# GeGLU feed-forward on one core: the first token block's transposes move from TensorE to the DMA queues

## The chip, the cores and the metric

The kernel runs on one core of a Trainium2 chip. The metric is device time in microseconds (us) for one execution; a time is the median of several runs. The core has a matrix engine (TensorE, PE in the profile, with its weight loads shown as PEld), a vector engine (VectorE, DVE), a scalar engine (ScalarE, ACT), a general one (GpSimd, POOL), and a synchronising engine (SyncE, SP) that here does nothing but issue DMA transfers. ScalarE issues DMA transfers as well, on a queue of its own.

## The reference

```python
B, S, D, F = 1, 2048, 1024, 3584          # all bfloat16
def reference(x, w_gate, w_up, w_down):
    return (gelu(x @ w_gate) * (x @ w_up)) @ w_down    # gelu: tanh approximation
```

x is 2048 tokens by 1024; w_gate and w_up are 1024 by 3584; w_down is 3584 by 1024.

## The kernel before

**Tiling.** The tokens are worked on in two halves of 1024 (`h`), each of two blocks of 512 tokens (`tb`). For the first two matrix products TensorE needs x transposed: `xT[tb]` holds, for each of the eight blocks of 128 input columns (`kd`, `KD` = 8), 128 partitions by 512 tokens. The 3584 hidden columns are taken as 28 blocks of 128, in 14 pairs; a chunk of weights has 512 of them, for w_gate (`j` = 0) and w_up (`j` = 1). The gated result goes to `hT`, which the down product reads.

**Most of the work is Winograd's form of a 2 by 2 block product**: seven products m1 to m7 instead of eight. Its sums of weights (`s1` to `s4`, made by `s_sum`, mostly on GpSimd) and of inputs (`t1` to `t4`, made by `t_sum`, mostly on VectorE) are kept in a 4-byte format. `quads` does this for the gate and up products (matmuls on line 418) and `down_group` for the down product (line 698).

**The very first pair is done the plain way**, because the sums are not there yet: `first_pair_units` runs 32 matmuls for the first token block and 32 for the second (`part`, which calls `mm_gu`, line 267), eight blocks `kd` times two matrices times two units `u`. Their weights are the first 256 columns (`FA`) of the first chunk. Then `quads` follows with pair 1, in the order in which it is written.

**How the first data come in.** `load_x0` (line 166) brings the first token block in rows: column quarters 0 and 1 of four (`XQ` = 256 columns), as three transfers. `transpose_x0` (line 311) turns these into `xT[0]` blocks 0 to 3 with 16 transposes of 128 by 128 on TensorE against an identity matrix, into PSUM banks, and VectorE (line 319) and ScalarE (line 321) copy them out. Blocks 4 to 7 of `xT[0]`, and all of `xT[1]`, come by transposing DMA transfers (`load_xT`, line 171). `load_w` (line 160) loads weights on SyncE's or ScalarE's queue.

**What sets the order.** The helpers `sp`, `act`, `dve`, `pool` and `pe` tie each engine's instructions to the order in which the program writes them, so each queue can be read off the text. Transfers signal on a small set of completion counters that are used in turn; a transfer whose counter is still in use by an earlier one waits for that one to land. Ahead of all real work TensorE runs `NWARM` matmuls of constants (`warm`, line 202), 128 by 512 each, to no purpose but to be busy.

The order of the first transfers is, on SyncE: half of x quarter 0, w_gate blocks 0 and 1, w_up blocks 0 and 1, w_up blocks 2 to 4, then transposing transfers of block 4, block 5 and blocks 6 and 7 of the first token block, then three of the second token block, then the rest of the first weight chunk and the second chunk. On ScalarE: the other half of x quarter 0, x quarter 1, w_gate blocks 2 to 4, and then w_gate and w_up blocks 5 to 7, which are tied behind the first transposing transfer; behind them the load of the table for gelu (line 225).

In `first_pair_units` the plain matmuls are interleaved with the transposes: eight transposes, half a warm-up, the gate matmuls of blocks 0 and 1 (four), eight transposes, the up matmuls of blocks 0 and 1 (four), and then blocks 2 to 7 in order.

Of the kernel before, what the change touches and what calls it, by code (L numbers as in the profile page):

```python
# [7 lines left out]

ACT = mybir.ActivationFunctionType
ALU = mybir.AluOpType  # L10
BF16 = mybir.dt.bfloat16
F32 = mybir.dt.float32
F32R = mybir.dt.float32r
SCHED_DEP = mybir.DependencyInfo(
    mybir.DependencyClass.NoSync, mybir.DependencyReason.SCHED_ONLY
)
# [18 lines left out]
def kernel(  # L35
# [8 lines left out]
    nc = tc.nc  # L44
    P = 128
    x2 = x.flatten_outer_dims()
    out2 = out.flatten_outer_dims()
    S, D = x2.shape
    F = w_gate.shape[1]
    KD = D // P  # L50
    KH = KD // 2
    KF = F // P
    TB = 512
# [3 lines left out]
    FG = 512  # L57
# [1 line left out]
    DN = 512  # L59
    NDN = D // DN  # L60
    TSB = TB // P
    XQ = 256
    NXQ = D // XQ
    KPQ = XQ // P
    NWARM = 7
    NPAIR = KF // 2
    PPG = FPG // 2
    WDT = 2
# [8 lines left out]
    wuv = w_up.rearrange("(ko ki) f -> ki ko f", ki=P)  # L77
    wdv = w_down.rearrange("(ko ki) d -> ki ko d", ki=P)

    const_pool = ctx.enter_context(tc.tile_pool(name="const", bufs=1))  # L80
    xT_pool = ctx.enter_context(tc.tile_pool(name="xT", bufs=1))
    shared_pool = ctx.enter_context(tc.tile_pool(name="shared", bufs=1))
    hT_pool = ctx.enter_context(tc.tile_pool(name="hT", bufs=1))
# [15 lines left out]
    CH = KD * FG  # L99
    w_mem = shared_pool.tile([P, 4 * CH + (NS - 4) * DN], BF16, name="w_mem")  # L100
# [5 lines left out]
    banks = [psum.tile([P, TB], F32, name=f"bank{i}") for i in range(8)]  # L106
    PB, VB, QB, RB = (0, 1), (2, 3), (4, 5), (6, 7)
    last_on = {}

    def on(engine, inst):  # L110

        if engine in last_on:
            tc.add_manual_dep(
                inst.ins, last_on[engine].ins.name, SCHED_DEP, reason="engine order"
            )
        last_on[engine] = inst
        return inst

    def sp(inst):
        return on("sp", inst)  # L120

    def act(inst):
        return on("act", inst)

    def dve(inst):
        return on("dve", inst)
# [12 lines left out]
    def pe(inst):  # L139
        return on("pe", inst)  # L140


    xs0 = w_mem[:, 4 * CH : 4 * CH + TSB * D].rearrange("p (a b) -> p a b", b=D)
    chunks = {}

    def new_chunk(key):
        c0 = 2 * CH * (key[1] % 2)
        chunks[key] = tuple(
            w_mem[:, c0 + j * CH : c0 + (j + 1) * CH].rearrange(
                "p (a b) -> p a b", b=FG  # L150
            )
            for j in range(2)
        )

    def load_w(key, j, k0, k1, queue=sp, f0=0, f1=FG):

        c0 = key[1] * FG
        eng = nc.scalar if queue is act else nc.sync
        src = (wgv, wuv)[j][:, k0:k1, c0 + f0 : c0 + f1]
        queue(eng.dma_start(out=chunks[key][j][:, k0:k1, f0:f1], in_=src))  # L160

    def load_x0(q, queue, ts0=0, ts1=TSB):
        eng = nc.scalar if queue is act else nc.sync
        cols = slice(q * XQ, (q + 1) * XQ)
        src = x2[ts0 * P : ts1 * P, cols].rearrange("(ts p) d -> p ts d", p=P)
        queue(eng.dma_start(out=xs0[:, ts0:ts1, cols], in_=src))

    def load_xT(xT, h, tb, k0, k1):
        t0 = h * SH + tb * TB
        sp(  # L170
            nc.sync.dma_start_transpose(
                out=xT[tb][:, k0:k1, :],
                in_=xv[t0 : t0 + TB, k0:k1, :],
            )
        )
# [4 lines left out]
    xT = [None] * NTB  # L180
# [3 lines left out]

    FA = 2 * P
    first = (0, 0)
    load_x0(0, sp, 0, 2)
    load_x0(0, act, 2, TSB)
    load_w(first, 0, 0, 2, sp, 0, FA)
    load_x0(1, act)  # L190
    load_w(first, 1, 0, 2, sp, 0, FA)
    load_w(first, 0, 2, 5, act, 0, FA)
    load_w(first, 1, 2, 5, sp, 0, FA)
    ident = const_pool.tile([P, P], BF16, name="ident")
    make_identity(nc, ident[:])

    warm_l = nc.const_aps.tensor(1.0, [P, P], BF16)
    warm_r = nc.const_aps.tensor(1.0, [P, TB], BF16)
# [1 line left out]
    def warm(bank, n=TB):  # L200
        pe(
            nc.tensor.matmul(  # L202
                banks[bank][:, 0:n],
                lhsT=warm_l,
                rhs=warm_r[:, 0:n],
                start=True,
                stop=True,
            )
        )

    for i in range(NWARM):
        warm(i)

    load_xT(xT, 0, 0, KH, KH + 1)
    behind_transpose = last_on["sp"]
    load_xT(xT, 0, 0, KH + 1, KH + 2)
    for j in range(2):
        load_w(first, j, 5, KD, act, 0, FA)
        tc.add_manual_dep(
            last_on["act"].ins,  # L220
            behind_transpose.ins.name,
            SCHED_DEP,
            reason="engine order",
        )
    act(nc.scalar.preload_act_table(ACT.Gelu_apprx_tanh))
    load_xT(xT, 0, 0, KH + 2, KD)
    for k0, k1 in ((0, 2), (2, KH), (KH, KD)):
        load_xT(xT, 0, 1, k0, k1)
    for j in range(2):
        load_w(first, j, 0, KD, sp, FA, FG)  # L230
    new_chunk((0, 1))
    for j in range(2):
        load_w((0, 1), j, 0, KD)


    tsum = {}
# [4 lines left out]
    def t_sum(name, c0=0, c1=KH, on_pool=False):  # L241
        def b(j, l):
            return xT[l][:, j * KH + c0 : j * KH + c1, :]

        t0 = ("t1", "t2", "t3", "b22", "t4").index(name) * KH * TB
        t = t_mem[:, t0 : t0 + KH * TB].rearrange("p (a b) -> p a b", b=TB)
        tsum[name] = t
        t = t[:, c0:c1, :]
        if name == "b22":
            for c in range(c1 - c0):  # L250
                act(nc.scalar.copy(out=t[:, c, :], in_=b(1, 1)[:, c, :]))
            return
        in0, in1 = {
            "t1": lambda: (b(0, 1), b(0, 0)),
            "t2": lambda: (b(1, 1), tsum["t1"].bitcast(F32)[:, c0:c1, :]),
            "t3": lambda: (b(1, 1), b(0, 1)),
            "t4": lambda: (b(1, 0), tsum["t2"].bitcast(F32)[:, c0:c1, :]),
        }[name]()
        if on_pool:
            pool(nc.gpsimd.tensor_tensor(out=t, in0=in0, in1=in1, op=ALU.subtract))  # L260
            return
        dve(nc.vector.tensor_tensor(out=t, in0=in0, in1=in1, op=ALU.subtract))


    def mm_gu(ps, w_sb, fi, tb, kd):
        pe(
            nc.tensor.matmul(  # L267
                ps[:],
                lhsT=w_sb[:, kd, fi * P : (fi + 1) * P],
                rhs=xT[tb][:, kd, :],  # L270
                start=(kd == 0),
                stop=(kd == KD - 1),
            )
        )
# [24 lines left out]
    def unit_out(hT, bset, fi, tb):  # L299
        mult(hT, gelu(banks[bset[0]]), banks[bset[1]], fi, tb)  # L300

    def transpose_x0(q):

        parts = [(2 * q, 0, 4), (2 * q + 1, 0, 4)]
        if q == 0:
            parts = [(0, 0, 2), (0, 2, 4), (1, 0, 4)]
        for n, (kd, ts0, ts1) in enumerate(parts):
            tp = banks[(PB + QB)[(2 * q + n) % 4]][:].bitcast(BF16)
            for ts in range(ts0, ts1):
                pe(  # L310
                    nc.tensor.transpose(  # L311
                        tp[:, ts * P : (ts + 1) * P],
                        xs0[:, ts, kd * P : (kd + 1) * P],
                        ident[:],
                    )
                )
            cols = slice(ts0 * P, ts1 * P)
            if q == 0 or n == 0:
                dve(nc.vector.tensor_copy(out=xT[0][:, kd, cols], in_=tp[:, cols]))
            else:  # L320
                act(nc.scalar.copy(out=xT[0][:, kd, cols], in_=tp[:, cols]))

    def part(held, tb, k0, k1, us=(0, 1), js=(0, 1)):
        for kd in range(k0, k1):
            for j in js:
                for u in us:
                    mm_gu(banks[held[u][j]], chunks[first][j], u, tb, kd)

    def first_pair_units(hT):

        held = (VB, RB)
        transpose_x0(0)
        warm(RB[1], TB // 2)
        part(held, 0, 0, KPQ, js=(0,))
        transpose_x0(1)
        part(held, 0, 0, KPQ, js=(1,))
        part(held, 0, KPQ, KD)
        t_sum("t1", 0, KH // 2)
        t_sum("t1", KH // 2, KH)
        for u in range(2):  # L340
            unit_out(hT, held[u], u, 0)
        held = (QB, PB)
        part(held, 1, 0, KH)
        t_sum("t2")
        t_sum("b22")
        t_sum("t3", 0, KH // 2)
        part(held, 1, KH, KD, (0,))
        unit_out(hT, held[0], 0, 1)
        t_sum("t3", KH // 2, KH)
        part(held, 1, KH, KD, (1,))  # L350
        unit_out(hT, held[1], 1, 1)
        for j in range(2):
            s_sum(0, 1, j, "s3", True, False)
        for name in ("s1", "s2", "s4"):
            for j in range(2):
                s_sum(0, 1, j, name)
# [711 lines left out]
```

## Time and profile before

| | |
|---|---|
| median of three runs | 539.03 us (538.97 to 539.69) |
| span of the profiled execution | 537.4 us |
| what lies around the span, if that execution took the median | 1.6 us |
| TensorE busy | 533.6 us, 99% |
| VectorE, ScalarE, GpSimd busy | 367.6, 263.5, 252.2 us |
| first warm-up matmul starts | 0.77 us |
| first plain matmul (line 267) starts | 4.93 us |
| first Winograd matmul (line 418) starts | 19.66 us |

A line of the chain has a start and a length in us, the engine, the tile and the line of the kernel, and how many instructions were merged. A line of the timeline has start, length, engine, line, operation, what is written and read, shapes and count; in brackets stands the idle time ahead and what ended it. A source line of a transfer has the duration of issuing it (smallest, median, largest, in ns) and when it was issued; "to landing" is from the start of the issue to the last completion. A line of a queue has packets, MB and busy share; q1 is SyncE's queue and q10 ScalarE's.

### The profile page before, as it was taken

The page shows a single profiled execution, that of the slowest core. Times are in us where ns is not written, and L with a number is a line of the kernel's source. Part 1 is how long each engine was busy: PE and PEld are TensorE (multiplying, and loading weights), DVE is VectorE, ACT ScalarE, POOL GpSimd, SP SyncE. Part 2 cuts the span into 40 slices and gives each one's busy share as a digit, 9 for nine tenths or more (in the row PEclk, how much of TensorE's full clock was granted, in tenths as well). Part 3 has the DMA queues.
Part 4 walks back from the last instruction along what each step waited for, and adds up shares of the span by engine and source line. Part 5 has one row for each costly group of instructions (what it writes and reads, how often), then busy time and mean ns, then how long its engine had stood idle before and what let it go on. Part 6 is the DMA issues. An engine that isn't in the chain of part 4 may idle for free.

```text
span 537.4 us, 7033 instructions
## 1 busy us (share of the span) xinstructions
PE 533.6 (99%) x2388; PEld 379.2 (71%) x2388; DVE 367.6 (68%) x476; ACT 263.5 (49%) x447; POOL 252.2 (47%) x213
## 2 busy tenths in 40 slices
PE   9999999999999999999999999999999999999997
PEld 4568686867677686777768676776768686866866
DVE  2985868787876998989555353444444669979961
ACT  2555555556465329117465554656555551452280
POOL 0698696969696200000056494958677670000000
PEclk9999999999999999999999999999999999999999
DMA  9965759697623887788950413314040329677846
GB/s 220 329 199 134 267 164 304 182 320 199 229 53 143 318 288 243 243 292 292 329 168 12 145 62 97 110 48 154 3 156 22 136 84 337 228 237 250 292 143 212
DMA packets 92547, 102.70 MB, mean 191 GB/s; under 512 B 18656, under 2 KB 67424, under 8 KB 92512
## 3 DMA queue, kind: packets, MB, share of 16 engines
q1 hardware_dynamic: 69568, 80.23, 45.7%
q10 hardware_dynamic: 22944, 22.02, 13.2%
q8 instruction: 19, 0.31, 0.3%
q14 instruction: 16, 0.13, 0.1%
HBM read 85.98 MB, written 12.58 MB: 183 GB/s over the span
## 4 chain that ended last, share of the span: by engine, by line
PE 99%; ACT 0%; issue 0%
PE bank L418 63%; PE bank L698 33%; PE bank L267 3%; PE bank L202 1%; PE bank L311 0%; ACT o_sb L754 0%
## 5 line engine op out<-in xcount | busy, mean ns | idle before, releaser
L418 PE MATMUL bank<-t_mem,s_mem 128*128 128x512 f32 x1056 | 244.6, 392 | 0.0
L418 PEld LDWEIGHTS bank<-t_mem,s_mem 128*128 128x128 f32 x1056 | 198.1, 188 | 42.7 <-issue 0.2
L388 POOL TENSOR_TENSOR s_mem<-w_mem 128x512 fp32r<-128x512 bf16 x102 | 124.0, 1236 | 185.5 <-DMA out_dram<-o_sb 96.9
L698 PE MATMUL bank<-t_mem,s_mem 128*128 128x512 f32 (+1 forms) x548 | 127.2, 391 | 0.0
L698 PEld LDWEIGHTS bank<-t_mem,s_mem 128*128 128x128 f32 x548 | 102.5, 188 | 22.0
L291 DVE TENSOR_TENSOR hT<-w_mem,bank 128x512 bf16<-128x512 f32 x106 | 72.5, 687 | 66.5 <-PE bank L418 44.5
L434 DVE TENSOR_TENSOR bank<-bank,m 128x512 f32<-128x512 f32 x108 | 70.0, 694 | 56.1 <-ACT m L472 54.3
L418 PE MATMUL bank<-xT,w_mem 128*128 128x512 bf16 x432 | 95.7, 379 | 0.0
L286 ACT ACTIVATE w_mem<-bank 128x512 f32<-128x512 f32 x106 | 63.0, 597 | 64.1 <-DVE bank L434 34.8
L418 PEld LDWEIGHTS <-w_mem 128*128 128x128 bf16 x432 | 41.2, 98 | 51.3 <-issue 3.4
L388 POOL TENSOR_TENSOR s_mem<-w_mem,s_mem 128x512 fp32r<-128x512 bf16 x52 | 68.4, 1335 | 2.9 <-PE bank L418 2.9
L600 DVE TENSOR_TENSOR t_mem<-w_mem 128x1024 fp32r<-128x1024 bf16 x56 | 65.9, 1225 | 0.9 <-PE bank L418 0.9
L388 POOL TENSOR_TENSOR s_mem<-s_mem,w_mem 128x512 fp32r<-128x512 f32 x52 | 61.3, 1200 | 0.0
L401 ACT CAST s_mem<-w_mem 128x512 fp32r<-128x512 bf16 x54 | 33.2, 616 | 31.3 <-PE bank L418 30.1
L478 ACT COPY bank<-bank 128x512 f32<-128x512 f32 x54 | 30.8, 570 | 26.6 <-PE bank L418 26.6
L670 DVE TENSOR_TENSOR s_mem<-hT 128x512 fp32r<-128x512 bf16 x52 | 36.7, 745 | 7.1 <-PE bank L698 7.1
L472 ACT COPY m<-bank 128x512 f32<-128x512 f32 x54 | 31.8, 589 | 18.4 <-PE bank L418 18.4
L698 PEld LDWEIGHTS <-hT 128*128 128x128 bf16 x224 | 21.3, 98 | 26.6 <-issue 2.1
L444 ACT COPY bank<-bank 128x512 f32<-128x512 f32 x54 | 30.7, 570 | 14.3 <-PE bank L418 13.5
L625 DVE TENSOR_TENSOR o_sb<-wd_sb,o_sb 128x512 fp32r<-128x512 bf16 x28 | 32.9, 1176 | 0.5
L763 ACT CAST o_sb<-bank 128x512 bf16<-128x512 f32 x27 | 14.8, 585 | 33.8 <-PE bank L698 33.8
L597 ACT CAST t_mem<-w_mem 128x1024 fp32r<-128x1024 bf16 x28 | 26.9, 1047 | 0.0
(46 smaller groups left out, 236.5 us busy)
## 6 DMA issues: line engine op xcount, KB each, us to landing
t_mem<-t_dram SPq DMA_DIRECT2D x56, 512.0 KB, 5.3
w_mem<-in_w_gate_dram ACTq DMA_DIRECT2D x10, 1024.0 KB, 5.4
w_mem<-in_w_up_dram ACTq DMA_DIRECT2D x10, 1024.0 KB, 8.3
wd_sb<-in_w_down_dram SPq DMA_DIRECT2D x28, 256.0 KB, 5.4
t_dram<-o_sb SPq DMA_DIRECT2D x28, 256.0 KB, 3.5
wd_sb<-in_w_down_dram SPq DMA_DIRECT2D x12, 512.0 KB, 7.6
w_mem<-in_w_down_dram SPq DMA_DIRECT2D x4, 1024.0 KB, 6.7
w_mem<-in_w_down_dram SPq DMA_DIRECT2D x8, 512.0 KB, 8.3
```

What stands on the lines that cost most here:

```text
L286: act(nc.scalar.activation(out=g_sb, in_=ps[:], func=ACT.Gelu_apprx_tanh))
L291: nc.vector.tensor_tensor(out=hT[:, fc, tb * TB : (tb + 1) * TB], in0=g_sb, in1=ps[:], op=ALU.mult,)
L388: pool(nc.gpsimd.tensor_tensor(out=t, in0=in0, in1=in1, op=op))
L401: act(nc.scalar.copy(out=t, in_=a(1, 1)))
L418: nc.tensor.matmul(banks[bank][:], lhsT=lhs[:, c, :], rhs=rhs[:, c, :], start=start and c == 0, stop=c == KH - 1, skip_group_check=True,)
L434: nc.vector.tensor_tensor(out=banks[dst][:], in0=banks[src][:], in1=m5[:], op=ALU.add)
L472: act(nc.scalar.copy(out=m5[j][:], in_=banks[V_[j]][:]))
L478: act(nc.scalar.copy(out=banks[R_[j]][:], in_=banks[Q_[j]][:]))
L600: dve(nc.vector.tensor_tensor(out=t, in0=in0, in1=in1, op=ALU.subtract))
L625: dve(nc.vector.tensor_tensor(out=t, in0=in0, in1=in1, op=ALU.subtract))
L670: dve(nc.vector.tensor_tensor(out=t, in0=in0, in1=in1, op=op))
L698: nc.tensor.matmul(banks[bank][:, c0:c1], lhsT=lhs(i, u), rhs=rhs(i)[:, c0:c1], start=start and i == 0, stop=stop and i == NS - 1, skip_gr ...
```

## The change

The transposes of x on TensorE are removed, with the row transfers of x, the identity matrix and the copies out of PSUM. All eight blocks of `xT[0]` come by three transposing transfers (blocks 0 and 1, blocks 2 and 3, blocks 4 to 7), and these are the first that SyncE issues. All six parts of the first weights are issued by ScalarE, and the load of the gelu table stands between the first and the second. The three transposing transfers of the second token block follow directly behind those of the first. There is one more warm-up matmul, and the half warm-up is gone. The plain matmuls run in one order, block by block.

```diff
-    NWARM = 7
+    NWARM = 8
...
-    load_x0(0, sp, 0, 2)
-    load_x0(0, act, 2, TSB)
-    load_w(first, 0, 0, 2, sp, 0, FA)
-    load_x0(1, act)
-    load_w(first, 1, 0, 2, sp, 0, FA)
-    load_w(first, 0, 2, 5, act, 0, FA)
-    load_w(first, 1, 2, 5, sp, 0, FA)
-    ident = const_pool.tile([P, P], BF16, name="ident")
-    make_identity(nc, ident[:])
+    for k0, k1 in ((0, 2), (2, KH), (KH, KD)):
+        load_xT(xT, 0, 0, k0, k1)
+    for k0, k1 in ((0, 2), (2, 5), (5, KD)):
+        for j in range(2):
+            load_w(first, j, k0, k1, act, 0, FA)
+            if (j, k0) == (0, 0):
+                act(nc.scalar.preload_act_table(ACT.Gelu_apprx_tanh))
+    for k0, k1 in ((0, 2), (2, KH), (KH, KD)):
+        load_xT(xT, 0, 1, k0, k1)
+    for j in range(2):
+        load_w(first, j, 0, KD, sp, FA, FG)
+    new_chunk((0, 1))
+    for j in range(2):
+        load_w((0, 1), j, 0, KD)
...
-    load_xT(xT, 0, 0, KH, KH + 1)
-    behind_transpose = last_on["sp"]
-    load_xT(xT, 0, 0, KH + 1, KH + 2)
-    for j in range(2):
-        load_w(first, j, 5, KD, act, 0, FA)
-        tc.add_manual_dep(
-            last_on["act"].ins,
-            behind_transpose.ins.name,
-            SCHED_DEP,
-            reason="engine order",
-        )
-    act(nc.scalar.preload_act_table(ACT.Gelu_apprx_tanh))
-    load_xT(xT, 0, 0, KH + 2, KD)
-    for k0, k1 in ((0, 2), (2, KH), (KH, KD)):
-        load_xT(xT, 0, 1, k0, k1)
-    for j in range(2):
-        load_w(first, j, 0, KD, sp, FA, FG)
-    new_chunk((0, 1))
-    for j in range(2):
-        load_w((0, 1), j, 0, KD)
...
-        transpose_x0(0)
-        warm(RB[1], TB // 2)
-        part(held, 0, 0, KPQ, js=(0,))
-        transpose_x0(1)
-        part(held, 0, 0, KPQ, js=(1,))
-        part(held, 0, KPQ, KD)
+        part(held, 0, 0, KD)
```

## The prediction

> **What bounds the kernel now.** I read the page first (engines, clock row, chain), then the chain of waits in order of time, the timeline of the first 25 us, the weight loads one by one, and the DMA landings and queues stretch by stretch.
>
> ```profile
> span 537.4 us, 7033 instructions
> PE 533.6 (99%) x2388; PEld 379.2 (71%) x2388; DVE 367.6 (68%) x476; ACT 263.5 (49%) x447; POOL 252.2 (47%) x213
> PEclk9999999999999999999999999999999999999999
> PE 99%; ACT 0%; issue 0%
> ```
>
> PE is the bound from 0.77 us to the end; no wait of any length stands in its chain. So a microsecond won or lost before the first Winograd product (L418) moves the end by that microsecond: no later gap absorbs it, and a later PE gives DVE, POOL and the loads more slack, not less. The question is only when L418 starts, 19.66 us in the timeline. The chain of that stretch:
>
> ```profile
> 0.77 3.15 PE bank L202 x7
> 3.92 0.85 PE bank L311 x8
> 4.77 0.21 PE bank L202
> 4.98 1.44 PE bank L267 x4
> 6.42 0.45 PE bank L311 x8
> 6.87 12.95 PE bank L267 x60
> ```
>
> The 60 matmuls take 12.95/60 = 0.2158 us each; the four before the second transposes take 1.44/4 = 0.36. The page's clock row shows 9 from the start and hides this; the single weight loads show it:
>
> ```profile
> 1.16 0.15 PEld L202 LDWEIGHTS <-const-bfloat16-1.0 128*128 128x128 bf16 x1 [0.28 <-issue]
> 2.86 0.15 PEld L202 LDWEIGHTS <-const-bfloat16-1.0 128*128 128x128 bf16 x1 [0.28 <-issue]
> 5.34 0.15 PEld L267 LDWEIGHTS <-w_mem 128*128 128x128 bf16 x1 [0.28 <-issue]
> 5.76 0.15 PEld L267 LDWEIGHTS <-w_mem 128*128 128x128 bf16 x1 [0.27 <-issue]
> 6.04 0.65 PEld L311 LDWEIGHTS <-w_mem 128*128 128x128 bf16 x8
> ```
>
> From 1.16 to 2.86 there are four steps, 0.425 us each; 5.34 to 5.76 is another; the next is 0.28, later ones 0.216. So PE runs at half speed until about 5.9 us, which is 5.1 us after its first matmul, without a pause before it. Check of the stretch: first L267 at 4.93, plus 64 x 0.2158 = 13.81, plus 0.45 for the second eight transposes, plus 0.47 for the matmuls at half speed, is 19.66. That is what the change works on.
>
> **Removed.** Sixteen PE transposes (L311) and the half-width warm-up: the first eight and the warm-up (0.85 + 0.21) lie ahead of the first real matmul, the second eight cost 0.45 behind it. Four DVE copies (L319), one ACT copy (L321) and the identity on POOL are off the path: DVE waited 4.5 us for a transpose afterwards, POOL 16.0 us for weights. Three x loads leave the queues. The eighth warm-up adds one of 0.425: warm-ups end at 0.77 + 8 x 0.425 = 4.17.
>
> **Added: the wait for x.** The first real matmul now waits for the first transposing load (T1, two 128-column blocks of x) and the first w_gate part. How transposing loads behave:
>
> ```profile
> L171 SPq DMA_TRANSPOSE xT<-in_x_dram x6: 1216/1552/2274, 2.8 to 10.3; - x6
> DMA to landing us min/median/max: 4.0/4.7/5.5
> DMA to landing us min/median/max: 2.6/2.6/2.6
> ```
>
> The first two lines are the six at the start, the last a lone one-block load at 73.9 us. Lower bound for T1: 2.6 plus 0.45 for a second block's 512 packets, issued at 0.74, lands at 3.8. Upper bound: the slowest two-block load, 5.5, lands at 6.2. Between them decides what else moves. The DMA queues at 8.8 to 9.6 us (first two lines, the transposing load in q1, ScalarE's weights in q10) and at 12.8 to 13.9 (transposing alone):
>
> ```profile
> q10 hardware_dynamic: 321, 0.16, 70.9%
> q1 hardware_dynamic: 328, 0.08, 47.7%
> q1 hardware_dynamic: 1242, 0.32, 127.4%
> ```
>
> Columns are packets, MB, busy share. Side by side the queues move equal numbers of packets, but a transposing packet carries 256 B and a weight packet 512: the transposing load gets 328/0.8 = 410 packets per us instead of 1242/1.1 = 1129. The change puts exactly these two side by side from the first microsecond. The Trainium skill ("DMA: Bandwidth & Descriptors", arbitration paragraph) says each DMA engine takes turns between queues packet by packet; the equal counts, 321 and 328, agree.
>
> In this profile the first packets move at 1.8 us, one queue alone until 2.4 (126 packets there; a lone transposing load in its ramp does some 250 in half a microsecond). So T1 has 250 of its 1024 by 2.4, the other 774 at 410 per us by 4.3, and lands about 0.6 us behind its last packet (0.5 to 0.9 in these six): **4.9 us**. w_gate's first 128 KB (256 packets, about 0.65 us) are there before. PE therefore stands idle from 4.17 to 4.9, while the clock is still low.
>
> **Moved.** SyncE's three transposes take about 1.55 + 1.55 + 2.27 to issue, so the second token block's follow at 6.2 (7.13 before), and the two big weight loads behind them at 11.6 (12.64): a microsecond earlier, where DVE (4.5 us) and POOL (16.0 us) waited for them. Nothing gained, since neither ends on the path. The built order shows that SyncE's fourth to sixth transposes wait for counters of loads landed before their turn, and that ScalarE's sixth weight part waits for T1 (4.9): it lands about 8, needed after 9. The activation table load, 1.28 us, stands behind ScalarE's first load. Its row at 6.11 shows no queue behind it; between holding back nothing and a whole 1.28 us I take nothing, since ScalarE's sequencer went on to a semaphore at 6.9, inside that load. If it holds all, w_up's first part lands about 6.9 against a need at 6.6: 0.3 us.
>
> T2 (blocks 2, 3) and T3 (blocks 4 to 7): ScalarE's first five parts are 1664 packets, at 321/0.8 = 401 per us from 2.4 to 6.55. T2 ends its packets about 6.5, lands 7.1. Of 4096 transposing packets 250 + 1700 are then done; 390 go beside ScalarE's last 384 (0.95 us), the other 1756 alone (1.56 us): 9.06, landing **9.65**. Lower bound by issue plus the four-block load's 4.5: 8.3; upper, with the longest landing lag and a pause of 0.6 between transposing loads like the one after 6.5 us: 10.6.
>
> **Forecast (0.50): slower, by the clock.** The only full-speed start in the trace followed 5.1 us of unbroken work. I take the break at 4.17 as starting that count again: half speed until 4.9 + 5.1 = 10.0, 5.1/0.425 = 12 matmuls in it, the other 52 at 0.2158 = 11.22, so L418 starts at 21.22, which is 1.56 us later. T2 is needed at 8.3 and T3 at 10.9, both landed. Span 537.4 plus 1.6 around it is the median 539.03; plus 1.56 is **540.6**. With T1 from 4.6 to 5.4 this case alone is 540.3 to 541.1. The Trainium skill ("TensorE: Matmul & The Clock Gate", the section on the HAM clock gate) says that a free-running window of about 3.4 us must be busy before the clock opens. By that rule a window broken at 4.17 counts only at the next, 5.9 + 3.4 = 9.3, and the time would be 540.25; 5.1 us lies between one window and two, so the trace agrees, but how much idle a window forgives no run here shows.
>
> **Rival 1 (0.28): the clock opens at 5.9 all the same.** For it: a gap of 0.7 us is small against 5.1. Against: the trace has no opening over a broken stretch, and the unbroken one took all of 5.1 us. Sixteen matmuls end at 8.85 and T3 decides: 9.65 + 48 x 0.2158 = 20.01, 0.35 later: 539.4 (538.6 with T3 at 8.3, 540.3 with T3 at 10.6).
>
> **Rival 2 (0.12): not slower, x comes in time.** It decides at T1 by 4.17 and T3 by 8.5. For it: the bounds 3.8 and 8.3. Against: the packet sharing. PE is gapless, clock open at 5.9: 4.1 matmuls at half speed, 59.9 x 0.2158 = 12.93, L418 at 18.83, that is 0.83 earlier: 538.2. Even this is 0.15%; a gain over 0.2% needs an earlier clock besides.
>
> **Rival 3 (0.10): T1 late.** At its upper bound of 6.2, with the clock counted from there: 6.2 + 5.1 + 11.22 = 22.52, 2.86 later: 541.9.
>
> That the change does not do what it says is excluded: the built order has no PE transposes, and T1 to T3 are first on SyncE.
>
> **Numbers.** Predicted 540.6. The range 539.0 to 541.9 reaches from rival 1 with a prompt T3 to rival 3; left out are rival 2, the low end of rival 1, and anything later than 6.2. 0.2% is 1.08 us, about what a measurement of this kernel can tell from no change (the three runs spread over 0.72). Slower: 0.50 + 0.10 + 0.02 of rival 1 = 0.62. Faster: 0.03, rival 2 with luck of the clock. Same: 0.35.
>
> **What would show it.** In the profile after: a gap on PE before the first L267-like matmul, ended by the transposing load, 0.4 to 1 us long; weight-load steps of 0.42 us past 6 us; ScalarE's and SyncE's queues equal in packets from 2.4 to 6.5; the first Winograd product near 21.2. Steps of 0.216 from about 6 us on would mean rival 1, no gap rival 2. A gap on PE anywhere after 25 us would make the whole sum wrong.

## The result and the profile after

The changed kernel takes 542.74 us (median of four runs, 541.84 to 543.63) against 539.31 before on the same chip: ratio 1.0065, 95% interval 1.0048 to 1.0081. On another chip (control run below) the ratio was 1.0048, interval 1.0033 to 1.0063. It is slower, by about twice what was forecast, and the time lies 0.8 us above the range.

The profiled execution took 541.84. Lines of the change moved up in the file: 239 is the plain matmul (267 before), 364 the Winograd matmul of `quads` (418), 159 the transposing load (171), 154 the weight load (160), 195 the warm-up (202). From the page:

```profile
span 540.1 us, 6984 instructions
PE 532.5 (99%) x2372; PEld 377.8 (70%) x2372; DVE 367.5 (68%) x472; ACT 262.9 (49%) x446; POOL 249.6 (46%) x211
```

PE is busy 1.1 us less and the span is 2.7 us longer. The chain of the first 30 us, in order of time, no longer runs on PE alone:

```profile
3.48 8.29 DMA xT<-in_x_dram
11.77 0.04 issue
11.81 10.52 PE bank L239 x48
22.33 7.83 PE bank L364 x35
```

It runs through the third transposing load, issued at 3.48 and landed at 11.77, and then through 48 matmuls. The timeline of PE shows the three waits, each ended by a transposing load:

```profile
4.92 1.89 PE L239 MATMUL bank<-xT,w_mem 128*128 128x512 bf16 x8 [0.58 <-DMA xT<-in_x_dram]
8.29 1.89 PE L239 MATMUL bank<-xT,w_mem 128*128 128x512 bf16 x8 [1.48 <-DMA xT<-in_x_dram]
11.81 10.52 PE L239 MATMUL bank<-xT,w_mem 128*128 128x512 bf16 x48 [1.64 <-DMA xT<-in_x_dram]
```

Here 11.81 + 48 x 0.2158 = 22.17 us is when the first Winograd matmul starts (22.17 in the timeline), 2.51 us later than before. That is nearly all of the 2.7. No later gap of PE takes it back: from the first Winograd matmul to the end it is 517.9 us, 517.7 before.

The transposing loads, all six of the start and then the second and the third alone (issue in ns, then from issue to landing):

```profile
L159 SPq DMA_TRANSPOSE xT<-in_x_dram x6: 1285/1328/5366, 0.7 to 11.6; - x6
DMA to landing us min/median/max: 3.7/4.3/8.3
DMA to landing us min/median/max: 6.1/6.1/6.1
DMA to landing us min/median/max: 8.3/8.3/8.3
```

The third took 5.37 us to issue and 8.3 to land; before, the longest of any of these was 2.27 and 5.5. Stretch by stretch (from and to, length, busy time of PE, PEld, DVE, ACT and POOL with instructions, clock, DMA share and, last, GB/s):

```profile
1.80:4.60 2.80, 2.55 (x6) 0.76 (x5) 0.00 (x0) 0.68 (x1) 0.00 (x0) 1.00 1.09 244
4.60:7.80 3.20, 1.89 (x8) 0.78 (x8) 0.00 (x0) 0.00 (x0) 0.00 (x0) 1.00 1.19 193
1.80:10.90 9.10, 6.32 (x22) 2.31 (x21) 0.00 (x0) 0.68 (x1) 0.00 (x0) 1.00 1.18 231
```

And the kernel before, to the end of the same bytes:

```profile
1.80:9.90 8.10, 8.10 (x41) 3.89 (x40) 1.35 (x4) 1.87 (x2) 0.00 (x0) 1.00 1.12 261
```

The same 2 MB (first token block and first weights; before, half of that token block came as plain rows) took 9.1 us at 231 GB/s after, 8.1 us at 261 before, and the worst stretch, 193 GB/s, is the one in which the second transposing load shares the queues with the weights.

Of the four runs two took 541.8 and 542.0 and two 543.5 and 543.6, these with a mean granted clock of 0.997 instead of 1.0 (0.003 x 541.7 = 1.6 us, as if it had been at half speed for some 3 us; no trace shows where).

### The profile page after: what moved, and what is told of

It is laid out like the page before. It is cut to its first block, busy times and chain, and to the rows that moved or that the text cites. A ratio compares the mean times of both kernels' runs of the same rounds, so it can differ in the third digit from the quotient of the medians.

```text
span 540.1 us, 6984 instructions
## 1 busy us (share of the span) xinstructions
PE 532.5 (99%) x2372; PEld 377.8 (70%) x2372; DVE 367.5 (68%) x472; ACT 262.9 (49%) x446; POOL 249.6 (46%) x211
## 4 chain that ended last, share of the span: by engine, by line
PE 97%; DMA 2%; SPq 0%; ACT 0%; issue 0%
PE bank L364 63%; PE bank L644 33%; PE bank L239 2%; DMA xT<-in_x_dram 2%; SPq L159 0%; ACT o_sb L700 0%
## 5 line engine op out<-in xcount | busy, mean ns | idle before, releaser
L546 DVE TENSOR_TENSOR t_mem<-w_mem 128x1024 fp32r<-128x1024 bf16 x56 | 68.2, 1265 | 0.9 <-PE bank L364 0.9
L334 POOL TENSOR_TENSOR s_mem<-w_mem,s_mem 128x512 fp32r<-128x512 bf16 x52 | 66.6, 1303 | 3.4 <-PE bank L364 3.4
```

Source lines behind the costliest of these rows:

```text
L334: pool(nc.gpsimd.tensor_tensor(out=t, in0=in0, in1=in1, op=op))
```

## The experiments

**The changed kernel once more (the control)**, beside the last two experiments, as their measure.

> The changed kernel once more, on the same chip as the two others, as their measure: 541.8 to 543.6, in two groups about 1.7 apart, the upper one with a granted clock of 0.997.

542.13 (541.58 to 542.37), ratio 1.0048 (1.0033 to 1.0063), five runs in one group; the upper group that was expected did not show. The trace on PE:

```profile
5.09 3.57 PE L239 MATMUL bank<-xT,w_mem 128*128 128x512 bf16 x8 [0.75 <-DMA xT<-in_x_dram]
9.54 1.89 PE L239 MATMUL bank<-xT,w_mem 128*128 128x512 bf16 x8 [0.87 <-DMA xT<-in_x_dram]
12.16 10.52 PE L239 MATMUL bank<-xT,w_mem 128*128 128x512 bf16 x47 [0.74 <-DMA xT<-in_x_dram]
```

In this run the first eight matmuls go at half speed (3.57 us instead of 1.89): the clock opened late, as forecast, though nearer 8.6 than the forecast's 10.0. It cost nothing: they were done by 8.7 and the next data landed at 9.49. The start of the Winograd part is 12.16 + 10.36 = 22.52, set by the third load as before.

**Warm-ups up to the first landing (e1).**

```diff
-    NWARM = 8
+    NWARM = 10
...
-        warm(i)
+        warm(i % 8)
```

> Two warm-up matmuls more, ten instead of eight, so they end at 0.78 + 10 x 0.425 = 5.0, just past the landing of the first transposing load (4.88). If the runs near 543.6 are those in which the idle 0.6 us made the clock open a window later, the clock now opens by 7.6 in every run, all runs come out near 541.9 and the median falls by about 0.9. If their difference comes from the transfers, the median stays at 542.7 and the runs still spread up to 543.6.

541.87 (541.43 to 543.0), ratio 1.0055 (1.0042 to 1.0067), which overlaps both measurements of the changed kernel. No run at 0.997; but the control had none either, with eight, and one run here took 543.0 at a clock of 1.0. Inconclusive. The third load landed at 11.74 here, as without the edit.

**Without the later weights (e2).**

```diff
-    for k0, k1 in ((0, 2), (2, 5), (5, KD)):
+    for k0, k1 in ((0, 2),):
...
-                lhsT=w_sb[:, kd, fi * P : (fi + 1) * P],
+                lhsT=w_sb[:, kw, fi * P : (fi + 1) * P],      # kw = kd % 2 in the first pair
```

> The four weight loads of blocks 2 to 7 of the first pair are left out, and its matmuls take blocks 0 and 1 of the weights in their place (other values, same shapes), so that the transposing loads have nearly no company on the queues. Theory A (weights side by side slow the transposing loads): the second lands near 5.5 instead of 8.25, the third near 7.7 instead of 11.77, PE loses its two later gaps, first Winograd matmul near 19.2, 538.5 to 539.5. Theory B (transposing loads one behind the other are slow by themselves): landings near 8 and 11.5, time 541.9 to 543.6 as before the edit.

539.89 over ten runs, ratio 1.0014 (1.0001 to 1.0027): some three quarters of the loss is gone. The loads landed at 5.19, 6.19 and 8.62 (theory A said 5.5 and 7.7, theory B 8 and 11.5), and one wait is left on PE, the first:

```profile
0.74 4.45 DMA xT<-in_x_dram
5.23 9.01 PE bank L239 x41
```

So 768 KB of weights less bring the third load 3.15 us earlier. The ten runs fell into two groups, 538.6 to 539.3 and 540.5 to 541.6.

**The same with warm-ups to the end of that wait (e6).**

```diff
-    NWARM = 8
+    NWARM = 11
...
-        warm(i)
+        warm(i % 8)
```

> As in e2 the weights of blocks 2 to 7 are left out and blocks 0 and 1 used for them; and three warm-ups more, eleven, so that they end at 5.45, past the first landing (5.19). The e2 runs stood in two groups, 538.6 to 539.3 and 540.5 to 541.6. If the upper group is the clock opening one stretch later because of the idle 0.9 us, it is gone: all runs 538.7 to 539.6. If it comes from the transfers, both groups stay.

539.39, all ten runs from 538.72 to 539.79; ratio 1.0004 (0.9994 to 1.0013). The upper group is gone:

```profile
0.77 4.85 PE L195 MATMUL bank<-const-bfloat16-1.0 128*128 128x512 bf16 x11 [0.77 <-PEq L998]
5.42 14.45 PE L239 MATMUL bank<-xT,w_mem 128*128 128x512 bf16 x63
```

This fits the forecast's clock mechanism, where nothing hides it: with 0.9 us of idle PE at the start five of ten runs take 1.2 us or more longer than the other five, and with constant matmuls in the gap none does. It is inferred from the edit: the two kernels ran on two chips, and the one trace of the first is of its fastest run, in which the clock had opened in time. It is not what the change lost by.

**Plain rows in place of transposing loads (e3).**

```diff
-        load_xT(xT, 0, 0, k0, k1)
+        src = x2[0:TB, k0 * P : k1 * P].rearrange("(ts p) d -> p ts d", p=P)
+        sp(nc.sync.dma_start(out=dst, in_=src))      # dst: the same part of xT[0]
```

> The three loads of the first token block carry the same bytes at the same places in the queue, but as plain row transfers (512 and 1024 bytes each packet) without transposing, so the values in xT[0] are others. If transposing itself is what costs (256-byte packets, pauses between them), the third load lands by 8.5 and the time is 538.5 to 539.5. If the volume on two queues is what costs, whatever the kind, the third lands at 10 or later and the time is 540.5 to 542.7.

541.94 (540.46 to 542.14), ratio 1.0043 (1.0028 to 1.0058). Neither theory: the third load of x landed at 8.70, as for "transposing costs", but the time stayed. Something else took its place: the second token block's transposing loads were now issued from 2.33 on, and w_up's last part, issued at 6.08 behind the second of them, landed at 13.43. PE waited for that. The edit had moved more than it was to move, so the next pair keeps one order for both.

**Everything on one queue, transposing (e4) and plain (e7).** In the first, SyncE issues x and weights in turn; the second is the same with the three loads of x plain, as above.

```diff
-    for k0, k1 in ((0, 2), (2, KH), (KH, KD)):
-        load_xT(xT, 0, 0, k0, k1)
-    for k0, k1 in ((0, 2), (2, 5), (5, KD)):
-        for j in range(2):
-            load_w(first, j, k0, k1, act, 0, FA)
-            if (j, k0) == (0, 0):
-                act(nc.scalar.preload_act_table(ACT.Gelu_apprx_tanh))
+    act(nc.scalar.preload_act_table(ACT.Gelu_apprx_tanh))
+    for x_blocks, w_blocks in (((0, 2), (0, 2)), ((2, KH), (2, 5)), ((KH, KD), (5, KD))):
+        load_xT(xT, 0, 0, *x_blocks)
+        for j in range(2):
+            load_w(first, j, *w_blocks, sp, 0, FA)
```

> All first weights go on SyncE's queue, each pair of parts right behind its transposing load, so nothing runs side by side; bytes and kinds are the same. Theory A: first load lands near 3.9, w_up's first part near 5, 2 MB at 290 GB/s end near 9.5, first Winograd matmul near 20.3, about 539.7 (540.5 with a late clock). Theory B: the pauses around transposing loads remain, last landings at 11 or later, 541.5 or more.

> As e4, everything on one queue in the same order, but the three loads of the first token block carry their bytes as plain rows, not transposed (other values in xT[0]). If transposing is what made e4 slow, 2 MB of plain loads at 310 GB/s end near 8.7 and land by 9.3, first Winograd matmul at 19 to 19.5, 538.5 to 539.5. If it is the volume on one queue, the last landing stays near 13 and the time near 542.4.

Transposing: 542.46 (541.91 to 542.59), ratio 1.006 (1.0046 to 1.0073). Plain: 540.2 (539.59 to 541.77), ratio 1.0022 (1.0013 to 1.0031). The intervals are apart: with order and bytes alike, transposing costs about 2 us (2.3 by the medians, which are of two chips). PE's last wait in the chain with transposing loads is for w_up's last part:

```profile
9.62 3.44 DMA w_mem<-in_w_up_dram
13.10 4.27 PE bank L241 x19
```

and that wait with plain ones:

```profile
9.90 10.52 PE L245 MATMUL bank<-xT,w_mem 128*128 128x512 bf16 x47 [0.92 <-DMA xT<-in_x_dram]
```

The third load of x landed at 11.11 and 9.86, the last weights at 13.06 and 11.02. The issue is part of what transposing costs here: the third load of x held SyncE for 3.26 us, as plain rows for 0.49, so the last weights were issued at 9.62 instead of 5.02. So two queues are not the cause by themselves: one queue is no faster. And the plain loads were slower than expected too: their median lies 0.7 us above the expected 538.5 to 539.5. A number for a bound: with nothing ahead of it or beside it, the first transposing load landed at 3.94 (3.8 in the prediction).

**The other half of the change alone (e8)**: the kernel before, with all first weights on ScalarE's queue.

```diff
-    load_w(first, 0, 0, 2, sp, 0, FA)
+    load_w(first, 0, 0, 2, act, 0, FA)
     load_x0(1, act)
-    load_w(first, 1, 0, 2, sp, 0, FA)
+    load_w(first, 1, 0, 2, act, 0, FA)
     load_w(first, 0, 2, 5, act, 0, FA)
-    load_w(first, 1, 2, 5, sp, 0, FA)
+    load_w(first, 1, 2, 5, act, 0, FA)
```

> The kernel before with the other half of the change alone: the three weight parts on SyncE's queue go to ScalarE's, in the order in which TensorE needs them; rows of x and TensorE transposes stay. If the weights' queue carries part of the loss, w_gate's first part lands near 6 instead of 4.9 and the later parts a microsecond later: 540 to 541. If only the transposing loads do, 539.0 to 539.6.

542.01 (541.5 to 542.49), ratio 1.0055 (1.004 to 1.007): as much as the whole change, and more than either theory allowed. On PE:

```profile
7.58 0.62 PE L311 MATMUL bank<-ident,w_mem 128*128 128x128 bf16 x8 [1.39 <-DMA w_mem<-in_x_dram]
10.43 0.60 PE L267 MATMUL bank<-xT,w_mem 128*128 128x512 bf16 x2 [0.69 <-DMA w_mem<-in_w_up_dram]
11.38 11.38 PE L267 MATMUL bank<-xT,w_mem 128*128 128x512 bf16 x51 [0.34 <-ACT xT L321]
```

SyncE, rid of its weights, issued its transposing loads from 1.25 us on (2.77 before). x quarter 1 landed at 7.53 (5.68 before), w_up blocks 2 to 4 at 10.38, and the last parts of w_gate and w_up at 12.02 and 13.44 (8.54 and 10.52 before). These two were issued only at 8.50 and 8.91: the first waited for a completion counter that a transposing load (landed at 8.48) still held, the second stood behind it. PE's last wait is for neither, but for ScalarE's copy of the last transposes out of PSUM, and that had to wait for the same two issues and for the table load behind them:

```profile
9.45 0.09 ACT L225
9.53 1.21 issue
10.74 0.59 ACT xT L321
```

Here too the transposing loads stood ahead of data that were needed earlier; the loss does not need a transposing load that PE waits for. But its last step, the copy, is one that the changed kernel does not have, so these 2.7 us are not a share of the change's loss.

**The third load in two (e5).**

```diff
-    for k0, k1 in ((0, 2), (2, KH), (KH, KD)):
+    for k0, k1 in ((0, 2), (2, KH), (KH, KH + 2), (KH + 2, KD)):
         load_xT(xT, 0, 0, k0, k1)
```

> The third transposing load, four blocks, becomes two of two blocks. If the end is set by the third load landing whole (11.77) ahead of 48 matmuls, blocks 4 and 5 now land near 10 and only 40 matmuls stand behind the last landing: first Winograd matmul near 20.5, about 1.6 less, 540.3 (up to 542 with a late clock). Against it: ScalarE's sixth weight part then waits for the second transposing load (8.25) and may land at 12 or later; if that takes the third load's place, nothing is gained, 541.5 to 543.5.

542.3 (541.06 to 543.32), ratio 1.0067 (1.005 to 1.0084): no gain that shows in the median. In the profiled run (541.06) the two halves landed at 10.42 and 11.27 and no longer held PE up, but the second load landed at 8.99 instead of 8.25 and was the one PE waited for last, with 56 matmuls behind it, 55 of them in the two longest pieces of the chain (in the control it lands later still, at 9.49):

```profile
9.03 7.34 PE bank L239 x33
16.43 4.91 PE bank L239 x22
```

**w_up's last part earlier (f1).** ScalarE's third and fifth part become one transfer, so that the last one gets a counter sooner (one run).

```diff
-    for k0, k1 in ((0, 2), (2, 5), (5, KD)):
-        for j in range(2):
-            load_w(first, j, k0, k1, act, 0, FA)
+    for j, k0, k1 in ((0, 0, 2), (1, 0, 2), (0, 2, KD), (1, 2, 5), (1, 5, KD)):
+        load_w(first, j, k0, k1, act, 0, FA)
...
```

> ScalarE's third and fifth parts (w_gate blocks 2 to 4 and 5 to 7) become one transfer, so that its last part, w_up blocks 5 to 7, waits for w_gate's first landing (3.3) instead of the first transposing load's (4.9), and is issued near 3.5, at or just ahead of the third transposing load. If the two queues are served in the order of issue, that part now lands by 9.5 instead of 11.48 and the third transposing load stays at 11.5 to 12. If they take turns, w_up's last part, issued 1.4 earlier, comes 1.4 earlier or less and the third load is not later than 11.8 by more than chance.

541.71 in the one run. The part was issued at 3.48, a few ns ahead of the third transposing load, and landed at 9.69 (11.48 before the edit, issued at 4.90): 1.79 earlier for 1.43 of earlier issue. The third load landed at 11.59, no later than before, but the second at 9.37 instead of 8.25. This speaks for service in the order of issue across both queues, though it is one run and 9.69 is later than the 9.5 expected of that. So do the queues of the changed kernel at 9.0 to 10.2 us (first line, the only queue with packets) and at 10.3 to 10.7 (second line):

```profile
q1 hardware_dynamic: 1328, 0.34, 126.1%
q10 hardware_dynamic: 270, 0.14, 113.9%
```

ScalarE's last part had been issued at 4.90, and its queue held nothing else; yet its first packet moved at 10.28, when the third transposing load, issued at 3.48, moved its last data packets (10.32). That load landed only at 11.77; in this experiment, with no weights left behind it, its data ended at 10.89 and it landed at 11.59. So the order of the two hardly moves the third landing: in both runs all 2 MB have moved near 10.9. It is no fixed order of issue either: in the kernel before, w_up's last part, issued 0.38 us after a transposing load of half that size, took turns with it (321 and 328 packets at 8.8 to 9.6).

**All three together (f2)**: ten warm-ups, the third load in two, five weight transfers.

> All that helped, on the changed kernel: ten warm-ups, the third transposing load in two, five transfers of weights instead of six. If the three costs named (idle PE ahead of the clock, the third load whole, the last weights late) are the loss, the first Winograd matmul comes near 20.7 and the median falls to 540.3 to 541. The transfers' order of x first and transposed stays, so it does not reach 539.3. If one of the three only hides behind another, 541.5 to 542.5.

543.2 (542.8 to 543.85), ratio 1.0072 (1.0048 to 1.0095); the control beside it 542.13. A miss: nothing was won. In the profiled run (542.9) the second load landed at 9.79 and PE waited 2.26 us for it:

```profile
9.83 12.25 PE L238 MATMUL bank<-xT,w_mem 128*128 128x512 bf16 x55 [2.26 <-DMA xT<-in_x_dram]
```

9.83 + 56 x 0.2158 = 21.91, 0.6 earlier than in the control. Bytes moved ahead of one load are late in the next, but this is not why the run is slower than the control. It lost 1.4 us behind the first Winograd matmul (519.2 us from there to the end, 517.8 in the control), most of it in one wait of the down product for sums that come back from DRAM:

```profile
228.68 1.84 PE L643 MATMUL bank<-t_mem,s_mem 128*128 128x512 f32 x7 [1.01 <-DMA t_mem<-t_dram]
```

No other trace has PE idle for more than 0.11 us at a time after 15 us; whether the edit brought this wait about is not shown. Two of the four runs had a clock of 0.997 although ten warm-ups left only 0.27 us idle ahead of the first matmul in the trace; where the clock fell was not seen.

## Why the prediction was wrong

**The direction and the place were right.** PE is the bound, the loss lies ahead of the first Winograd matmul, and nothing gives it back. The first landing was computed as 4.9 and is 4.88, in part by luck: of the 250 packets that the sum gives the first load by 2.4 us none had moved, and then they came at 480 per us (1056 from 2.4 to 4.6) instead of 410. ScalarE's table load held back no transfer (1.20 to 2.48, the next issue at 1.23).

**The step that failed is the landing of the second and third transposing loads:** 7.1 and 9.65, upper bound 10.6, in the prediction; 8.25 and 11.77 in the profile, 9.49 and 12.12 in the control. The mechanism that set the time is the one written under rival 1, "T3 decides", with the end at T3 + 48 x 0.2158. With 11.81 in place of 9.65 it gives 22.17, to the hundredth. What made the landings late is shown in part: the weights beside them (e2) and the transposing (e7 against e4).

**The mis-sized term is the rate.** The prediction made 2 MB out of packet rates read in stretches of 0.8 and 1.1 us in which the queues ran without a pause; its sum, from 1.8 to 9.06, comes to 2.1 MB / 7.26 us = 289 GB/s. Measured were 231, to 10.9; that is 1.8 of the 2.1 us by which the third landing was missed, and the rest is that it came 0.9 behind this end instead of 0.6. The kernel before had 261 for the same bytes: there they landed at 10.8. That landing was in the trace of before, and 10.8 as the landing of the third load would by itself have given 21.2.

Over longer stretches transposing loads keep some 230 GB/s even nearly alone: in e2, between landings 5.19 and 13.11, 1.75 MiB in 7.92 us are 232 GB/s; there SyncE issued the six loads one right behind the other from 0.74 to 10.79, so the issuing may set this rate as well as the transposing, and no run tells the two apart. Kind and company both cost: on one queue, plain rows in the same order gained about 2 us, and leaving out 768 KB of weights won back three quarters of the loss. A slip in the sum is small beside this: the prediction lets the second load end its packets at 6.5 with 1950 of 2048 moved; at 410 per us it is 6.8. Why the stretch from 4.6 to 7.8 runs at 193 GB/s when a mixture of the same kinds ran at 310 in the kernel before (8.8 to 9.6) stays open.

**A second error was the model of the queues.** The equal packet counts at 8.8 to 9.6 us were read as queues taking turns. The Trainium skill ("DMA: Bandwidth & Descriptors", arbitration paragraph) says that an engine takes turns between the queues it has work for, and equal counts do appear where two loads were issued close together. But where the prediction named equal counts as a sign, they did not come: 682 packets on ScalarE's queue and 1056 on SyncE's from 2.4 to 4.6, 727 and 1056 from 4.6 to 7.8. And a load issued 1.42 us behind a long transposing one on the other queue had no turn until that was through: 1328 packets to none. SyncE's issues also came later than computed, the fourth transposing load at 8.89 instead of 6.2, since the third held its issue for 5.37 us instead of 2.27. That cost nothing by itself.

**The forecast itself, the clock, was the wrong bound.** In the profiled run the clock was open at 4.92 in spite of the break: eight weight loads in 1.61 us. In the control it opened late and the lost time disappeared in the wait for the second load. The runs of e2 and e6 speak for the mechanism where data come early, where it takes 1.2 us or more from half of the runs; here data came late. The Trainium skill's rule ("TensorE: Matmul & The Clock Gate", section on the HAM clock gate), a free-running window that must be busy, fits runs that fall on either side of it by chance. The traces bear it out, and not the prediction's count of 5.1 us.

In every one of the 13 traces the recorded clock stays at full speed for 532.48 or for 535.89 us, 3.41 apart, as if it changed only at the ends of windows of that length. In the profiled run it opened at 4.81, behind a window with 2.95 us of matmuls; in the control a window ended at 5.18 with 2.66 and the clock stayed low until 8.59. Counted back from each opening in steps of 3.41, the windows that opened it held 2.88 us or more in all 13, and none that left it low held more than 2.67. So the break alone does not decide; where the windows lie does too, and that differs from run to run.

**Where the bounds failed.** Each load had bounds of its own, and only the first load's upper bound was carried to the top of the range (541.9). The third load's upper bound of 10.6 was built on the same sum, with one pause of 0.6 us and the longest lag added; it was no bound.

## What to carry to other kernels

Before a start-up is priced by rates of single stretches, read from the trace when the same bytes last landed, and ask how much work stands behind that landing: before, the last data were needed with some 40 matmuls to go, after, with 48 and one microsecond later. Here, moving bytes between the queues or cutting a load in pieces shifted the lateness to another load while the sum of bytes ahead of the work stayed; what gained was fewer bytes and, on one queue, plain ones instead of transposing ones. A long transposing load issued early is not only late itself: here it stood ahead of weights that were issued after it on the other queue as well.

## What was not expected of the hardware

- A transposing load of 512 KB held SyncE's issue for 5.37 us when the queues were full (2.27 in the kernel before), and a 192 KB weight load on the other queue, issued 1.42 us after the start of that issue, moved its first packet 5.3 us after its own.
- A break of PE of 0.58 us did not keep the clock from opening in the profiled run (full speed from 4.92); with one of 0.75 us, in the control, all of the first eight matmuls ran at half speed.
- The change's second half alone, which alters no transposing load and moves three weight loads to the other queue, cost 2.7 us: the transposing loads were issued 1.5 us earlier by it, and a copy on ScalarE came later.
